# A layer of recurrent-memory attention and SwiGLU on one core: earlier stack loads, an up sum in SBUF, and x operands split anew

## The chip, the cores and the metric

The kernel runs on one core of one Trainium2 chip, as one launch. The metric is the device time of that launch in microseconds. The core has the engines PE (TensorE, with its weight loader PEld), DVE (VectorE), ACT (ScalarE), POOL (GpSimd) and SP, which here only issues DMA transfers. All transfers of this kernel are issued by SP, in program order. Every engine works through its own list of instructions in order and waits on semaphores. Tiles lie in SBUF, the results of matmuls in eight banks of PSUM.

## The reference

The input x has 2048 rows of D = 576. Two branches are mixed by a gate of each row:

```python
g = _sigmoid((x * gate_w).sum(-1, keepdims=True))
a = _A_ref(x, A_wq, A_wk, A_wv, A_wo, A_beta)
b = _B_ref(x, B_w_gate, B_w_up, B_w_down)      # (silu(x @ w_gate) * (x @ w_up)) @ w_down
return g * a + (1 - g) * b
```

The attention branch has 32 heads of 18 and 4 segments of 512 rows. In each segment a head does causal softmax attention inside the segment and reads a memory matrix of the earlier segments:

```python
logits = einsum(qs, ks) * scale + mask;  a_dot = softmax(logits) @ vs
a_mem = (phi(qs) @ M) / (phi(qs) @ z + 1e-6)
o = g * a_mem + (1 - g) * a_dot
M = M + phi(ks).T @ vs;  z = z + phi(ks).sum()
```

The SwiGLU branch goes from 576 to 4608 = 36 x 128 and back. All is in float32.

## The kernel before, in words

**Number formats.** A float32 operand is split into a high part and the rest (`split`, L106: a copy on ACT, a subtraction on DVE), and a product is three matmuls of such parts. In attention, q and k are split into three bfloat16 parts, which are stacked along the contracted dimension.

**Three stages.** The first (L263 to L574) does the projections, segment by segment: `qk` (9 chains each), `v_step` and the memory. What it makes is stored to DRAM: the stacked q and k (`stk`), v (`vd`), the memory's part (`med`). It also stores, for segments 0 and 1, the split operands of x: four tiles of high and low part in segment 0, two in segment 1 (`xd`, L547, six stores of 128x1024 float32) and the remainder rows (`xsd`). The third stage (from L1045) does the output projection and the mixture.

**The second stage** interleaves two things by hand. The outer loop (L942) runs over 72 blocks: two halves of the rows (the first half takes segments 2 and 3, the second segments 0 and 1) by 36 blocks of 128 hidden columns. Between the products of a block stands `tick()`, eight to a block, which calls `beat`. A beat first runs what `defer` put down for it (`due`: loads, splits, stores), then up to three groups of the down product (`down_group`), then, when enough credit has been gathered, one step of attention (`next(att)`).

**A block's gate and up product** (L984 to L1019) use a scheme with seven products in place of eight: each of `XO[0]` to `XO[6]` is one operand of x, a block of x or a sum of such blocks, split in high and low part, of two tiles z = 0, 1 (hence fourteen). Three PSUM banks hold the sums: `a` (bank 0), `xx` (bank 1), `y` (bank 2). The rows `p5`, `sg0` and `sg1` are SBUF tiles of 128x512 from a pool of four. The first up block is added on DVE at L994 (into bank 2, on which PE goes on), the second at L1011 (again a new tile in bank 2). At the block's end `sg1` (second block: up sum times Silu of the gate) is multiplied at L1015 and `sg0` at L1016, where `xx` comes straight from PE. The next block's first product goes to bank 0, its copy to bank 1 and its second product to bank 2. The rows are then split to `hh`, `hl` (L1017, L1018), the operands of the down product. Every third block starts 48 groups of the down product over the last three blocks; each is nine matmuls of 288 columns into one of two banks, and a DVE addition into `ya` (L788).

**Attention steps.** `att_gen` (L713) runs 64 units (a segment and a pair of heads) of five steps. Step n of unit u does `s_bank(u, n)` (scores for the maximum, L619, reduced on DVE, L626), and for a unit two to three before it `t_bank` (L659, scores again with the maximum stacked in; exponential on ACT, L663; mask on POOL, L671), then a split of the probabilities (`p1` on DVE, L737, `p2` on POOL, L739) and `pv_step` (L688, L690). A unit's stacked q and k are ten loads (`stack_loads`, L171) into one of four buffers `qst`, `kst`: the first six bring what step 0 of the unit reads, the last four (pr = 1) what step 1 reads besides. They are issued for unit u + 1 in steps 2, 3 and 4 of unit u, three, three and four of them (L723). The row maxima go through DRAM: stored in step 3 (`mxd`, L720), loaded two units later in step 0 (`row_load`, L188).

**Weights.** In the first half each block's weights are loaded raw, summed and split (`w_make`), and stored (`wc`, `rc`); in the second half `w_fetch` loads them split (L599, L603).

**Between the halves** stand ten beats with the last 16 groups. From block 34 on, `x_second` (L890) makes the operands of the second half: eight raw tiles of x are loaded (L897) into a pool of four buffers, four operands for each z are summed on POOL in place (`total`) and split (`parts`), and three for each z (0, 3, 5, the plain blocks of x) are loaded split from `xd` (`kept`, L911). The remainder rows come from `xsd` (`rest`, L915). Each entry has the beat at which it runs, counted from the first tick of block 35.

Of the kernel before, what the change touches and what calls it, by code (L numbers as in the profile page):

```python
# [12 lines left out]
F32 = mybir.dt.float32  # L13
# [7 lines left out]
P = 128  # L21
# [4 lines left out]
L = 512  # L26
# [25 lines left out]
def f32(ap):  # L52
    return ap.bitcast(F32)
# [3 lines left out]
def gated_mix(ctx, tc, xT, wf, wd, wv, wo, beta, cmask, ident, bmask, out):  # L57
# [11 lines left out]
    mxd = dram.tile([2 * NB, 3, 8, P], BF, name="mxd")  # L69
    wc = dram.tile([FT, 7, P, 4 * P], F32, name="wc")  # L70
    rc = dram.tile([FT, 2, P, 2 * P], F32, name="rc")
    xd = dram.tile([2, 4, P, 2 * L], F32, name="xd")
    xsd = dram.tile([2, P, L], F32, name="xsd")
    dc = dram.tile([FT, P, 2 * D], F32, name="dc")
    ffd = dram.tile([8, P, D], F32, name="ffd")
# [30 lines left out]
    def split(hi, lo, src):  # L106
        nc.scalar.activation(hi, src, AF.Copy)  # L107
        nc.vector.tensor_sub(lo, src, f32(hi))  # L108
# [154 lines left out]
    with ExitStack() as st:  # L263
# [228 lines left out]
        for s in range(NSEG):  # L492
# [47 lines left out]
            for n in range(8):  # L540
                hf, i = divmod(n, 4)
                flush()
                v_step(s, hf, i)
                if s:
                    mem_step(s, n // 2, n % 2)
                if s < 2 and n > 1 and n - 2 in ((0, 1, 2, 3), (2, 3))[s]:
                    late.append((xd[s, n - 2], f32(xs_of[s][0][n - 2]).rearrange("p a b -> p (a b)")))  # L547
                if s < 2 and n == 6:
                    late.append((xsd[s], f32(xs_of[s][1])))
                if s < 3:  # L550
                    if n == 0:
                        xs_of[s + 1] = x_tiles(s + 1)
                    if 1 <= n < 6:
                        x_split(xs_of[s + 1], n - 1, raws["x", n - 1])
                else:
                    if n == 4:
                        wraw_of[1] = [w_load(1, u) for u in range(2)]
                    if n < 2:
                        first_sum(6, n)
                    elif n < 6:  # L560
                        nc.gpsimd.memset(kst[n - 2], -1.0)
                    else:
                        nc.gpsimd.memset(mbs[n - 6], 0.0)
                    if n > 2:
                        for z in stack_loads(0)[2 * n - 6:2 * n - 4]:
                            nc.sync.dma_start(*z)
                    for _ in range((0, 0, 2, 3, 3, 3, 3, 3)[n]):
                        if start[0][0] < 8:
                            start.pop(0)[1]()
# [7 lines left out]
    with ExitStack() as st:  # L577
# [135 lines left out]
        def att_gen():  # L713
            N = 10 * NB
            for tau in range(N + TL + VL + 4):
# [4 lines left out]
                    nc.sync.dma_start(mxd[u - 1].rearrange("z q n -> q z n"), mts.pop(u - 1))  # L720
                if n == 0 and 2 <= u <= 2 * NB + 1:
                    row_load(u - 2)
                if n > 1 and u + 1 < 2 * NB:  # L723
                    for d in stack_loads(u + 1)[(0, 3, 6)[n - 2]:(3, 6, 10)[n - 2]]:
                        nc.sync.dma_start(*d)  # L725
                z = tau - TL - VL - 1
                if z % 20 == 0 and 0 <= z < N and z // 20 + 1 < 4 * NSEG:
# [162 lines left out]
        def x_second(new, xs):  # L890
            r = {}
            todo = []

            def load(z, q):
                b, kt = ((0, z), (1, z), (0, 2 + z), (1, 2 + z))[q]
                r[z, q] = raw_tile()[:, :L]
                nc.sync.dma_start(r[z, q], xT[HALF[1][b], :, kt])  # L897

            def total(z, j):
                c, d, e, g = (r.get((z, q)) for q in range(4))  # L900
                o, p, q = {1: (c, d, c), 4: (d, g, d), 2: (g, g, c), 6: (e, e, g)}[j]
                nc.gpsimd.tensor_sub(o, p, q)

            def parts(z, j):
                new[j][z] = x_slot(SLOT[j], z)
                split(new[j][z][:, 0], new[j][z][:, 1], r[z, {1: 0, 4: 1, 2: 3, 6: 2}[j]])

            def kept(z, j):
                b, kt = {0: (0, z), 3: (0, 2 + z), 5: (1, 2 + z)}[j]
                new[j][z] = x_slot(SLOT[j], z)  # L910
                nc.sync.dma_start(f32(new[j][z]).rearrange("p a b -> p (a b)"), xd[b, kt])  # L911

            def rest(b):
                xs[b] = xs_tile()
                nc.sync.dma_start(f32(xs[b]), xsd[b])  # L915

            for z, loads, sums, splits in ((0, (-3, -2, 5, 4), (4, 7, 8, 8), (5, 9, 9, 10)),
                                           (1, (9, 10, 12, 11), (13, 13, 14, 14), (14, 15, 15, 16))):
                todo += [(o, lambda z=z, q=q: load(z, q)) for o, q in zip(loads, range(4))]
                for o, p, j in zip(sums, splits, (1, 4, 2, 6)):  # L920
                    todo += [(o, lambda z=z, j=j: total(z, j)), (p, lambda z=z, j=j: parts(z, j))]
                todo += [(o + z, lambda z=z, j=j: kept(z, j)) for o, j in ((6, 0), (12, 3), (14, 5))]
            todo += [(16 + b, lambda b=b: rest(b)) for b in range(2)]
            return sorted(todo, key=lambda t: t[0])

        def seven(t, w, x, first, last):
# [15 lines left out]
        for pos, (half, f) in enumerate(seq):  # L942
# [64 lines left out]
            nc.scalar.activation(sg1, y, AF.Silu)  # L1007
            tick()
            rest2(a, wr[1], XS[1])
            y = y_tile()  # L1010
            nc.vector.tensor_add(y, a, p5)  # L1011
            tick()
            seven(xx, w[6], XO[6], False, False)
            rest2(xx, wr[1], XS[0])
            nc.vector.tensor_mul(sg1, y, sg1)  # L1015
            nc.vector.tensor_mul(sg0, xx, sg0)  # L1016
            defer(2, lambda t=(hh[:, 0], hl[:, 0], sg0): split(*t))  # L1017
            split_by(3, hh[:, 1], hl[:, 1], sg1)  # L1018
            tick()  # L1019
# [99 lines left out]
```

## Time and profile before

Three runs took 1901.53, 1901.6 and 1904.46 us; the median is 1901.6. The profile is of one more execution.

| | |
|---|---|
| median of three runs | 1901.6 us |
| the profiled execution | 1898.35 us |
| its span | 1896.5 us |
| mean granted PE clock | 0.995 |
| busy ACT and POOL | 958.4 and 854.6 us |
| DMA: moved, mean rate | 337.63 MB, 178 GB/s |
| share of 16 DMA engines, SP's queue | 54.0% |

The span runs from the first to the last instruction; the profiled execution's own time has 1.85 us more around it. Matmuls are pipelined and their ends are modelled, so a matmul of 512 columns shows 0.39 us and the next starts 0.23 us behind it. A row of a timeline has the start, the time until the end of the last of the merged instructions, engine, line, operation, output and input, the count, and in brackets how long the engine stood idle ahead of it and who ended that. A row of waits has the waiting engine, tile and line, the one waited for, the total in us, the number of times and the longest. "PEld" is the loader of PE's weights, which works ahead of the matmuls; "SPq" is the issue of a transfer.

By stage, the projections end at about 230 us, the first half runs to about 1027 us, the second to about 1806 us, and the output projection to the end.

### The profile page before, as it was taken

Reading aid. Unit: us, or ns where it says so; the run is one execution under the profiler, and the core shown is the slowest. Engines: PE = TensorE matmul, PEld = TensorE weight load, DVE = VectorE, ACT = ScalarE, POOL = GpSimd, SP = SyncE. Lnnn points to the kernel's source line nnn. Section 1 sums busy time; section 2 is a strip of 40 time slices with the busy share of each in tenths; the row PEclk is TensorE's granted clock in tenths of the full one; section 3 lists DMA queues with packets and bytes.
Section 4 is the critical chain, followed back from the end, with each engine's and each line's share of the span. In section 5 each row is a group of like instructions: output and inputs, shape, how many; then the busy total and the mean of one; then the engine's idle time right before and its main releaser. Section 6 shows DMA issues by size and latency. Waiting matters only on the chain.

```text
span 1896.5 us, 36496 instructions
## 1 busy us (share of the span) xinstructions
PE 1820.1 (96%) x12508; PEld 1544.5 (81%) x12508; DVE 1217.4 (64%) x3026; ACT 958.4 (51%) x1778; POOL 854.6 (45%) x1246
## 2 busy tenths in 40 slices
PE   8999999999999999999998999999999999999999
PEld 7889877887887888788777788878778878888899
DVE  5555677777767777877676566565556555655455
ACT  7666556456546656664663553544454354354311
POOL 3323623554555464555446454454444444444121
PEclk9999999999999999999999999999999999999999
DMA  6544586456446646654757653554464364445544
GB/s 237 197 171 167 186 282 216 146 190 227 155 162 224 209 150 204 229 171 145 234 178 255 196 169 112 165 167 131 144 186 138 120 194 145 136 149 155 191 151 137
DMA packets 206472, 337.63 MB, mean 178 GB/s; under 512 B 38416, under 2 KB 95888, under 8 KB 206288
## 3 DMA queue, kind: packets, MB, share of 16 engines
q1 hardware_dynamic: 206288, 335.32, 54.0%
q8 instruction: 99, 1.62, 0.4%
q14 instruction: 85, 0.70, 0.1%
HBM read 197.48 MB, written 137.76 MB: 177 GB/s over the span
## 4 chain that ended last, share of the span: by engine, by line
PE 70%; DMA 10%; DVE 7%; ACT 5%; issue 3%; SPq 3%; POOL 1%; DVEq 0%; ACTq 0%; POOLq 0%
PE bank L783 23%; PE bank L930 21%; PE bank L130 11%; PE bank L936 4%; PE bank L619 3%; PE bank L659 3%; DMA kst<-stk 2%; SPq L725 2%; PE bank L688 2%; DMA raw<-in_wf_dram 1%; PE bank L690 1%; DMA qst<-stk 1%; DMA qst<-mxd 1%; ACT L663 1%; DMA woraw<-in_wo_dram 1%
## 5 line engine op out<-in xcount | busy, mean ns | idle before, releaser
L739 POOL TENSOR_TENSOR p<-pe,p 128x512 f16<-128x512 f32 x320 | 372.9, 1165 | 696.3 <-DVE p L737 607.6
L783 PE MATMUL bank<-dw,hh 128*128 128x288 f32 x2304 | 482.1, 302 | 11.4 <-DVE ya L788 7.4
L783 PEld LDWEIGHTS bank<-dw,hh 128*128 128x128 f32 x2304 | 378.7, 189 | 32.9 <-DVE ya L788 13.9
L663 ACT ACTIVATE pe<-bank 128x512 f32<-128x512 f32 x320 | 191.1, 597 | 356.5 <-PE bank L659 301.9
L783 PE MATMUL bank<-dw,hl 128*128 128x288 f32 x1152 | 340.7, 296 | 0.4 <-DVE hl L108 0.3
L788 DVE TENSOR_TENSOR ya<-bank,ya 128x288 f32<-128x288 f32 x352 | 160.1, 456 | 236.3 <-PE bank L783 234.1
L626 DVE CUSTOM_DVE_ANT_0 scr<-bank,cm 128x512 bf16<-128x512 f32 (+3 forms) x512 | 247.4, 483 | 23.3 <-PE bank L619 16.5
L783 PEld LDWEIGHTS bank<-dw,hl 128*128 128x128 f32 x1152 | 217.4, 189 | 0.8 <-DVE hl L108 0.8
L659 PE MATMUL bank<-qst,kst 111*128 111x512 bf16 (+3 forms) x512 | 151.6, 305 | 7.6 <-DMA qst<-mxd 7.6
L619 PE MATMUL bank<-kst,qst 108*128 108x512 bf16 (+3 forms) x512 | 126.4, 300 | 28.5 <-DMA kst<-stk 11.6
L737 DVE CAST p<-pe 128x512 f16<-128x512 f32 x320 | 151.8, 475 | 0.3 <-POOL pe L671 0.3
L671 POOL TENSOR_SCALAR_AFFINE_SELECT pe<-pe 128x256 f32<-128x256 f32 (+1 forms) x320 | 134.5, 420 | 15.2 <-ACT pe L663 12.5
L1011 DVE TENSOR_TENSOR bank<-bank,row 128x512 f32<-128x512 f32 x72 | 50.3, 699 | 108.3 <-ACT row L1007 107.7
L998 ACT ACTIVATE row<-bank 128x512 f32<-128x512 f32 x72 | 43.0, 597 | 132.6 <-PE bank L936 132.3
L663 ACT ACT_TABLE_LOAD x66 | 84.7, 1283 | 49.2 <-PE bank L659 48.3
L108 DVE TENSOR_TENSOR hl<-row,hh 128x512 fp32r<-128x512 f32 x72 | 50.3, 699 | 79.7 <-ACT hh L107 79.7
L130 PE MATMUL bank<-xo,qhi 128*128 128x512 f32 x288 | 92.3, 401 | 5.2 <-ACT xo L107 5.0
L619 PEld LDWEIGHTS <-qst 108*128 108x128 bf16 x512 | 50.3, 99 | 54.5 <-issue 34.1
L659 PEld LDWEIGHTS <-kst 111*128 111x128 bf16 x512 | 47.8, 97 | 50.0 <-issue 33.0
L1002 ACT ACTIVATE bank<-bank 128x512 f32<-128x512 f32 x72 | 41.9, 582 | 91.3 <-PE bank L930 87.8
L1004 ACT ACT_TABLE_LOAD x67 | 86.0, 1283 | 1.2
L320 POOL TENSOR_TENSOR q<-qr,q 128x512 bf16<-128x512 f32 x36 | 43.8, 1217 | 92.8 <-ACT q L319 86.1
(2085 smaller groups left out, 4230.5 us busy)
## 6 DMA issues: line engine op xcount, KB each, us to landing
raw<-in_wf_dram SPq DMA_DIRECT2D x72, 320.0 KB
dc<-dw SPq DMA_DIRECT2D x36, 576.0 KB
dw<-dc SPq DMA_DIRECT2D x36, 576.0 KB
stk<-q SPq DMA_DIRECT2D x32, 384.0 KB
draw<-in_wd_dram SPq DMA_DIRECT2D x36, 288.0 KB
vd<-vps SPq DMA_DIRECT2D x8, 912.0 KB
v<-vd SPq DMA_DIRECT2D x16, 456.0 KB
qst<-stk SPq DMA_DIRECT2D x128, 54.0 KB
```

Of the source, the lines that this page charges most:

```text
L130: nc.tensor.matmul(t, st[n], mv[n], start=(n == 0), stop=(n == 13))
L619: nc.tensor.matmul(t[:, c:c + w], qs[:KR, pr, P * i:P * i + P], ks[:KR, pr, 0:w], start=True, stop=True)
L626: nc.vector.tensor_tensor_reduce(scr[:, :w], t[:, c:c + w], cm[:, L - w:L], 1.0, -3.0e38, OP.add, OP.max, m[:, k:k + 1])
L659: nc.tensor.matmul(t[:, c:c + w], ks[:KR + 3, pr, P * j:P * j + P], qs[:KR + 3, pr, P * j:L], start=True, stop=True)
L663: nc.scalar.activation(pe, t, AF.Exp, scale=SCALE)
L671: nc.gpsimd.affine_select(d, d, pattern=pat, compare_op=OP.is_ge, fill=0.0, base=0, channel_multiplier=-1)
L737: nc.vector.tensor_copy(p1, pe)
L739: nc.gpsimd.tensor_sub(p2, pe, p1)
L783: nc.tensor.matmul(t, p, q[:, cs], start=(n == 0), stop=(n == 3 * CH - 1))
L788: nc.vector.tensor_add(ya[:, i, cs], t, ya[:, i, cs])
L930: nc.tensor.matmul(t, w[:, p, z], x[z][:, q], start=first and n == 0, stop=last and n == 5, skip_group_check=True)
L1004: nc.scalar.activation(sg0, sg0, AF.Silu)
```

## The change

Three edits, in one diff (whole but for context lines):

1. The ten stack loads of a unit are issued in two steps instead of three: six in step 2, four in step 3.
2. The second up block is summed in its own SBUF row (`p5`, in place of a new tile in bank 2), and at the block's end the product of `sg0` (gate times up from PE's bank) is made first, that of `sg1` second; the latter reads two SBUF rows.
3. The six stores to `xd` and the six loads from it are gone; operands 0, 3 and 5 of the second half are split from the raw tiles like the others. Their splits stand ahead of the sums that overwrite the raw tiles, the beats of sums and splits are set anew, three raw loads of z = 1 come one beat later, and the two remainder loads two beats earlier.

```diff
-    xd = dram.tile([2, 4, P, 2 * L], F32, name="xd")
...
-                if s < 2 and n > 1 and n - 2 in ((0, 1, 2, 3), (2, 3))[s]:
-                    late.append((xd[s, n - 2], f32(xs_of[s][0][n - 2]).rearrange("p a b -> p (a b)")))
...
-                if n > 1 and u + 1 < 2 * NB:
-                    for d in stack_loads(u + 1)[(0, 3, 6)[n - 2]:(3, 6, 10)[n - 2]]:
+                if n in (2, 3) and u + 1 < 2 * NB:
+                    for d in stack_loads(u + 1)[6 * (n - 2):4 * n - 2]:
                         nc.sync.dma_start(*d)
...
             def parts(z, j):
                 new[j][z] = x_slot(SLOT[j], z)
-                split(new[j][z][:, 0], new[j][z][:, 1], r[z, {1: 0, 4: 1, 2: 3, 6: 2}[j]])
-
-            def kept(z, j):
-                b, kt = {0: (0, z), 3: (0, 2 + z), 5: (1, 2 + z)}[j]
-                new[j][z] = x_slot(SLOT[j], z)
-                nc.sync.dma_start(f32(new[j][z]).rearrange("p a b -> p (a b)"), xd[b, kt])
+                split(new[j][z][:, 0], new[j][z][:, 1], r[z, (0, 0, 3, 2, 1, 3, 2)[j]])
...
-            for z, loads, sums, splits in ((0, (-3, -2, 5, 4), (4, 7, 8, 8), (5, 9, 9, 10)),
-                                           (1, (9, 10, 12, 11), (13, 13, 14, 14), (14, 15, 15, 16))):
+            for z, loads, steps in ((0, (-3, -2, 5, 4), ((1, -1, 0), (3, 1, 0), (4, -1, 1), (7, 4, 0), (7, -1, 5),
+                                                         (8, -1, 3), (8, 2, 0), (9, 6, 0), (9, -1, 4), (10, -1, 2),
+                                                         (10, -1, 6))),
+                                    (1, (9, 11, 13, 12), ((12, -1, 0), (13, 1, 0), (14, 4, 0), (14, -1, 1), (14, -1, 5),
+                                                          (15, 2, 0), (15, -1, 3), (15, -1, 4), (16, 6, 0), (16, -1, 2),
+                                                          (17, -1, 6)))):
                 todo += [(o, lambda z=z, q=q: load(z, q)) for o, q in zip(loads, range(4))]
-                for o, p, j in zip(sums, splits, (1, 4, 2, 6)):
-                    todo += [(o, lambda z=z, j=j: total(z, j)), (p, lambda z=z, j=j: parts(z, j))]
-                todo += [(o + z, lambda z=z, j=j: kept(z, j)) for o, j in ((6, 0), (12, 3), (14, 5))]
-            todo += [(16 + b, lambda b=b: rest(b)) for b in range(2)]
+                for o, j, k in steps:
+                    todo.append((o, lambda z=z, j=j: total(z, j)) if j > 0 else (o, lambda z=z, k=k: parts(z, k)))
+            todo += [(14 + b, lambda b=b: rest(b)) for b in range(2)]
...
             rest2(a, wr[1], XS[1])
-            y = y_tile()
-            nc.vector.tensor_add(y, a, p5)
+            nc.vector.tensor_add(p5, a, p5)
             tick()
             seven(xx, w[6], XO[6], False, False)
             rest2(xx, wr[1], XS[0])
-            nc.vector.tensor_mul(sg1, y, sg1)
             nc.vector.tensor_mul(sg0, xx, sg0)
+            nc.vector.tensor_mul(sg1, p5, sg1)
```

On PE the list of instructions stays as it is. DVE and ACT get six instructions more each, SP has twelve transfers fewer.

## The prediction

> **What bounds the kernel now.** I read the page first, then the waits of PE and of its weight loader, then the order of time around three places that the change touches.
>
> ```profile
> span 1896.5 us, 36496 instructions
> PE 1820.1 (96%) x12508; PEld 1544.5 (81%) x12508; DVE 1217.4 (64%) x3026; ACT 958.4 (51%) x1778; POOL 854.6 (45%) x1246
> ```
>
> The profiled execution took 1898.35 us, its span 1896.5 us and 1.85 us around it. PE is busy for 1820.1 us of that, and the change leaves its 12508 matmuls alone, so what can move are the 76.4 us in which PE waits. Who ends those waits (total us, times, longest):
>
> ```profile
> PE bank L619 <- DMA kst<-stk: 11.6, 11, 2.1
> PE bank L619 <- ACT pe L663: 10.9, 14, 2.1
> PE bank L659 <- DMA qst<-mxd: 7.6, 3, 6.5
> PE bank L783 <- DVE ya L788: 7.4, 8, 2.2
> ...
> PE bank L930 <- DVE bank L994: 4.3, 9, 1.1
> ...
> PE bank L619 <- DMA wc<-wo__11212: 3.4, 1, 3.4
> PE bank L930 <- DVE bank L1011: 3.0, 4, 1.5
> ...
> PE bank L619 <- DMA wo__20455<-wc: 1.8, 1, 1.8
> ...
> PE bank L619 <- ACT row L998: 0.7, 1, 0.7
> ```
> ```profile
> PEld bank L930 <- DVE bank L1011: 14.8, 26, 1.9
> ```
>
> No engine bounds the kernel as a whole beside PE; it is many small late arrivals. The largest is the stack (kst) that comes late to L619, and of those that the other two edits can reach, L1011 and the row load qst<-mxd are the next. 72 executions of the SwiGLU block, 36 to each half, share the time with 64 attention units of five steps.
>
> **The up row.** At the end of a block:
>
> ```profile
> 307.64 1.52 PE L930 MATMUL bank<-xo,wo__3382 128*128 128x512 f32 x6
> ...
> 308.38 0.58 ACT L1007 ACTIVATE row<-bank 128x512 f32<-128x512 f32 x1
> ...
> 308.99 0.70 DVE L1011 TENSOR_TENSOR bank<-bank,row 128x512 f32<-128x512 f32 x1 [2.00 <-ACT row L1007]
> 309.00 0.61 PE L936 MATMUL bank<-xs,wr__3385 128*128 128x512 f32 x2
> ...
> 309.75 1.66 PE L930 MATMUL bank<-xo,wo__3437 128*128 128x512 f32 x6
> ...
> 309.93 0.68 DVE L1015 TENSOR_TENSOR row<-bank,row 128x512 f32<-128x512 f32 x1
> ...
> 310.53 0.68 DVE L1016 TENSOR_TENSOR row<-bank,row 128x512 f32<-128x512 f32 x1
> ```
> ```profile
>   ACT row L1007: 107.7, 49
> ```
>
> L1011 writes its sum over the bank that the gate's Silu (L1007) still reads, so DVE stands there for 107.7 us in 49 blocks. The next block's first product overwrites bank 0, which L1011 reads, so PE waits for it too. Six matmuls take 1.52 us and two 0.61, so they follow each other by 0.23; behind the two of 309.00 L930 could start at 309.45 and starts at 309.75: 0.30 us lost. With the sum in its SBUF row, L1011 waits only for the matmuls into bank 0. They stand on PE right ahead of the product of 307.64, so they are done by about 307.9, a microsecond before the Silu; the sum then ends at 308.6 and no PE wait is left. The row is held to the block's end; the next to write its buffer is the next block's L998, behind three more products: nothing. Size: 3.0 us is all that shows as idle PE, 14.8 us as idle weight loader, which overstates because matmuls run on behind it. 26 cases: some sixteen like the one above at 0.30 make 4.8, two long ones (1.9 the longest) add 3. I take **-8**, range -3 to -15. What is late next is the gate times up: the first product waits for PE's last matmul as before, the second, which used to lie in front of it under PE's work, now comes behind it.
>
> **The stack loads.** SP issues loads for unit u+1 in steps 2, 3 and 4 of unit u, and L619 reads the last four in step 1 of u+1:
>
> ```profile
> 1195.79 0.29 SPq L720 DMA_DIRECT2D mxd<-mt  x1
> ...
> 1202.41 0.72 SPq L725 DMA_DIRECT2D qst<-stk  x1
> 1203.17 0.69 SPq L725 DMA_DIRECT2D kst<-stk  x1
> ...
> 1204.57 0.61 SPq L725 DMA_DIRECT2D kst<-stk  x1
> ```
> ```profile
> 1209.44 0.38 PE L619 MATMUL bank<-kst,qst 108*128 108x512 bf16 x1 [1.44 <-DMA kst<-stk]
> ```
>
> All ten wait at their start for the buffer, which L659 of step 1 reads last; six instead of three now stand behind that one wait. The last issue ends at 1205.18, PE is released 4.26 us later and had been ready 1.44 us before. After the change the four follow the mxd store of step 3. Steps 2 and 3 issue three and one more (0.7 us each), so mxd goes from 1195.79 to about 1198.0 and the four end near 1201.1; landed 4.26 us later, 1205.3, against 1208.0 when PE wants them: 2.7 us to spare. I take the 11 kst waits to be of this shape, and, as the same matmul waits in them, the 3.4, 1.8 and 0.7 us put down to weight transfers and to L998, which no L619 reads. Together 17.5; I take **-15**, range 0 (the queue of transfers, not the issue, sets the landing) to -17.5. What moves behind them: SP is in order, so weights, raw rows and row loads queued between come up to 2.2 us later. The slack of one such weight:
>
> ```profile
> 1182.42 0.36 SPq L599 DMA_DIRECT2D wo__15635<-wc  x1
> ```
> ```profile
> 1190.12 1.63 PE L930 MATMUL bank<-xo,wo__15635 128*128 128x512 f32 x6
> ```
>
> 7.3 us from the issue's end to its use, less 2.2 leaves 5.1, over the 4.26 of the stack. I charge **+1**, range 0 to 8.
>
> **Between the halves.** Six stores (0.5 MB each) in the projections and their six loads between the halves go; six splits come, one ACT and one DVE instruction each, and loads of raw x stay (three of them one step later).
>
> ```profile
> 992.24 1.00 SPq L911 DMA_DIRECT2D xo<-xd  x2
> ...
> 995.03 0.30 SPq L189 DMA_DIRECT2D qst<-mxd  x1
> ```
> ```profile
> 1002.63 0.58 PE L659 MATMUL bank<-qst,kst 111*128 111x512 bf16 x1 [6.51 <-DMA qst<-mxd]
> ```
> ```profile
> 990.00:1000.00 10.00, 4.00 (x23) 2.68 (x22) 5.67 (x10) 4.64 (x7) 3.92 (x4) 0.97 0.93 281
> 1000.00:1010.00 10.00, 7.37 (x41) 6.54 (x41) 6.95 (x17) 2.90 (x6) 7.83 (x12) 0.69 0.89 295
> ```
>
> The columns are length, PE, PEld, DVE, ACT, POOL busy, clock, DMA share, GB/s. The row load stands behind two xd loads, 1.05 MB at 281 GB/s: 3.7 us of its landing are theirs, so -3.7 of the 6.51. The stores fall in the projections (L130), for which the list of waits has no transfer: nothing. Against it, the splits:
>
> ```profile
> L108 DVE TENSOR_TENSOR xo<-raw,xo x8: 674/1002/1215, 991.0 to 1021.9; 128x512 fp32r<-128x512 f32 x8
> ```
>
> Six more at 1.0 us make 6.0 on DVE, which is busy 12.6 us of those 20, so they fit on average; but the adds of the down product (L788) free PE's two banks and stand in the same queue, and the new ACT splits stand ahead of the hh split, waiting for raw x. I charge +2.7: net **-1**, from -5 to +6.
>
> **The clock.** PE's granted clock falls after a wait:
>
> ```profile
> 862.00:866.00 4.00, 1.08 (x8) 0.99 (x9) 3.42 (x8) 0.50 (x2) 2.61 (x4) 1.00 0.84 285
> 866.00:870.00 4.00, 4.00 (x15) 3.33 (x14) 0.49 (x3) 0.25 (x2) 2.51 (x7) 0.57 0.49 181
> ```
>
> This is the 3.4 us wait, then 4 us at 0.57: 4 x 0.43 = 1.7 lost. That wait should go; the dip at 1000 to 1010 (0.69, 3.1 us, part of it while PE stood) may shorten. **-2**, range 0 to -5.
>
> **The price of the new product and its order.** The product of the up row now reads two SBUF rows. Rows for that:
>
> ```profile
> L1015 DVE TENSOR_TENSOR row<-bank,row x72: 677/685/692, 237.2 to 1803.5; 128x512 f32<-128x512 f32 x72
> ```
> ```profile
> L869 DVE TENSOR_TENSOR hl<-row,hh x72: 676/682/1224, 244.6 to 1806.3; 128x512 fp32r<-128x512 f32 x72
> ```
> ```profile
> 656.08 0.41 DVE L233 TENSOR_TENSOR wo__8285<-raw,wo__8285 128x256 fp32r<-128x256 f32 x1
> ...
> 656.97 1.16 POOL L739 TENSOR_TENSOR p<-pe,p 128x512 f16<-128x512 f32 x1 [1.57 <-DVE p L737]
> ...
> 657.36 1.06 DVE L233 TENSOR_TENSOR wo__8296<-ws,wo__8296 128x256 fp32r<-128x256 f32 x1
> ```
>
> From bank and row it took 677 to 692 ns in all 72 blocks; a subtraction of two SBUF rows has the same median, 682, but reached 1224. The same instruction took 0.41 us alone and 1.06 us while POOL's L739 ran, ending 0.29 us after it. So the new product costs 0.68 us, and up to 1.16 more where it meets POOL. DVE finishes the block's pair up to 0.68 later than today where it now waits for PE. That reaches PE only in the 24 blocks with down-product groups, whose adds follow; elsewhere DVE has the microsecond it gained at L1011. I charge **+1.5**; bounds 0 and 24 x (0.68 + 1.16) = 44.
>
> The Trainium skill, page "SBUF — State Buffer", section "Who interferes with whom", says that a DVE instruction with two SBUF inputs contends with a GpSimd instruction that reads SBUF, and that whoever comes second is blocked for the whole instruction. By that rule, the trace's 1.06 us agrees, and this edit moves an operation from the safe side to the other; it is the slower rival below.
>
> **The sum.** Waits removed come back in part: PE, no longer held, meets the next late one, chiefly the exponentials (ACT pe L663, 10.9 us, untouched). I give back a quarter of the row's and the stack's 23: +5.5, bounds 0 and 23. So -8 - 15 + 1 - 1 - 2 + 1.5 + 5.5 = **-18**. On the profiled execution's 1898.35 that is 1880.4; the median of the three runs, 1901.6, lies 3.25 above it, so 1883.6, say **1883.5 us**, 1.0% faster. Likeliest range 1875 to 1893. Under 0.2% (3.8 us) a measurement here can't tell from no change.
>
> **Rivals.**
> - *The waits move on*: the whole 23 returns at ACT's exponentials, or the stack lands no earlier because transfers queue (DMA share 0.93 in one stretch) and the row's -8 alone stays. The first gives -18 + 17.5 = -0.5, so 1901; the second -18 + 15 - 3.75 (its share of what was given back) + 1.7 (the clock dip stays), -5, so 1896.5. For it: 10.9 us of such waits at L619. Against: ACT is 51% busy, and the example has 2.7 us to spare. 0.16.
> - *DVE late behind the block's end* (slower): the new product, behind the one that waits for PE and blocked by POOL, delays the adds after it, so PE waits for its two banks. All 24 blocks at 1.84 make +44 for the +1.5: -18 + 42.5 = +24.5, so 1926. It decides against the change from (18 + 1.5) / 24 = 0.81 us per block. For it: 7.4 us of L783 waits for L788 today, and the 1.06 above. Against: the product of two rows has median 682, and POOL is 45% busy. 0.10.
> - *More than the sum*: nothing returns, the clock dips go, the boundary gains its 3.7: -8 - 17.5 - 3.7 - 5 = -34, so 1867. 0.08.
>
> **How the numbers follow.** Forecast 0.66. The first rival's 0.16 is 0.07 for 1896.5 (0.27% faster), 0.08 for 1901 and 0.01 above. So faster 0.66 + 0.08 + 0.07 = 0.81, within 0.2% 0.08, slower 0.10 + 0.01 = 0.11. The range, 1867 to 1899, leaves out the slower rival, the top of the first and little below.
>
> **What would show it.** Right: the kst wait of L619 near zero with loads in two groups of six and four; DVE's 107.7 us at L1007 gone and no PE wait for the up sum; PE's wait between the halves under 4 us. Wrong: the up product's median well over 700 ns or L788 waits over 15 us (second rival); L619's waits for ACT grown by ten (first); weights late at L930; a longer stretch between the halves. If the stack waits go but the time stays, my reading of L619 as PE's own loss is wrong.

## The result: 1880.8 us against 1901.6 us

| | before | after |
|---|---|---|
| median (runs) | 1901.57 us (4) | 1880.76 us (4) |
| lowest to highest | 1899.64 to 1904.46 | 1876.04 to 1885.42 |
| ratio, 95% interval | | 0.9889 [0.9861, 0.9917] |
| profiled execution, span | 1898.35, 1896.5 | 1885.42, 1883.6 |
| DMA moved | 337.63 MB | 331.34 MB |

The forecast was 1883.5 us and faster; the time lies 2.7 us below it and inside the range. Measured again beside the experiments, the same kernel took 1883.74 us, 0.9917 [0.9893, 0.994] of before. The profiled execution of after is the slowest of its four, so its trace shows 12.9 us of gain (1898.35 to 1885.42), not the 20.8 of the medians.

The page of after, its first lines:

```profile
span 1883.6 us, 36500 instructions
PE 1816.2 (96%) x12508; PEld 1548.4 (82%) x12508; DVE 1227.2 (65%) x3032; ACT 960.4 (51%) x1784; POOL 858.9 (46%) x1246
```

PE waits for 1883.6 - 1816.2 = 67.4 us, before 76.4: 9.0 less. Its busy time fell by 3.9 us as well, with the same 12508 matmuls. The list of PE's waits in after (total us, times, longest us):

```profile
PE bank L616 <- ACT pe L660: 14.9, 17, 2.7
PE bank L780 <- DVE ya L785: 12.6, 11, 3.4
PE bank L925 <- DVE bank L989: 9.2, 8, 1.8
...
PE bank L780 <- DVE hl L107: 2.6, 2, 1.4
...
PE bank L656 <- DMA qst<-mxd: 1.1, 2, 0.6
```

(After's lines are one to six lower: L616, L656, L660, L780 and L785 were L619, L659, L663, L783 and L788; L925, L931, L989 were L930, L936, L994; the sum is L1005, the gate's product L1009, the up product L1010.) The kst row, 11.6 us, is not there any more; the row load fell from 7.6 to 1.1. DVE's wait of 107.7 us for the Silu is gone too. What grew: the exponentials 10.9 to 14.9, L989 4.3 to 9.2, ya 7.4 to 12.6. The end of the block that the prediction took as its example, in order of time:

```profile
307.62 0.69 DVE L1005 TENSOR_TENSOR row<-bank,row 128x512 f32<-128x512 f32 x1 [0.57 <-PE bank L931]
...
308.44 0.58 ACT L1002 ACTIVATE row<-bank 128x512 f32<-128x512 f32 x1
...
308.78 0.62 PE L931 MATMUL bank<-xs,wr__3377 128*128 128x512 f32 x2
...
309.23 1.52 PE L925 MATMUL bank<-xo,wo__3430 128*128 128x512 f32 x6
...
309.70 0.68 DVE L1009 TENSOR_TENSOR row<-bank,row 128x512 f32<-128x512 f32 x1
...
310.30 0.68 DVE L1010 TENSOR_TENSOR row<-row 128x512 f32<-128x512 f32 x1
```

The sum now runs before the Silu (L1002), and the next block's first product starts 0.45 us behind the two matmuls of 308.78, not 0.75 as before. The 0.30 is gone, and it had never shown as idle PE but as a busy matmul. The product of two SBUF rows over all blocks:

```profile
L1010 DVE TENSOR_TENSOR row<-row x72: 675/681/1219, 237.7 to 1791.0; 128x512 f32<-128x512 f32 x72
```

Its median is 681 ns, as forecast, and 1219 its longest.

Between the halves, the row load's 6.51 us wait went (by which edit, e1 and e3 below show), and others stand there:

```profile
992.25 3.38 POOL L899 TENSOR_TENSOR raw<-raw 128x512 f32<-128x512 f32 x2
992.74 1.75 DVE L107 TENSOR_TENSOR xo<-raw,xo 128x512 fp32r<-128x512 f32 x1
...
992.87 0.61 PE L780 MATMUL bank<-dw,hl 128*128 128x288 f32 x1 [1.43 <-DVE hl L107]
...
996.55 1.83 DVE L107 TENSOR_TENSOR xo<-raw,xo 128x512 fp32r<-128x512 f32 x2
...
999.89 0.85 PE L780 MATMUL bank<-dw,hh 128*128 128x288 f32 x2 [3.37 <-DVE ya L785]
```
```profile
990.00:1030.00 40.00, 35.14 (x232) 30.91 (x231) 30.16 (x65) 11.39 (x23) 26.65 (x32) 0.80 0.51 169
```
```profile
990.00:1030.00 40.00, 30.20 (x226) 26.48 (x225) 27.02 (x59) 12.81 (x23) 23.51 (x27) 0.91 0.85 281
```

The columns are those of the prediction's windows; the first row is after's, the second before's. The transfers are lighter (DMA share 0.51, before 0.85). But PE waits 3.37 us for DVE's adds, which stand in the queue with the splits, and the granted clock of these 40 us is 0.80, before 0.91.

**The clock as a term of its own.** PE runs at full speed or, in short stretches, at half; the granted clock is the mean over the span. Each run lists its span and its mean granted clock. In four sets of runs of before the mean is 0.9944 (29 runs), 0.9943 (14), 0.9945 (17) and 0.9946 (8), so it belongs to a kernel and is not chance alone. I split each time into span x clock, called the time at full clock here, and the rest, the loss to the clock; both are means over all runs of a kernel, against before on the same chip. The standard error of a full-clock mean is 0.4 to 0.9 us (1.3 for the whole change), so a difference between two rows of the table is uncertain by about 1 us, more where the whole change is one of them.

| kernel | ratio of times, 95% | full clock, us | clock loss, us |
|---|---|---|---|
| e1 stack loads alone | 0.9952 [0.9935, 0.9968] | -10.2 | +0.2 |
| e2 row sum and gate first alone | 0.9963 [0.9948, 0.9979] | -6.7 | -0.2 |
| e3 x operands alone | 1.0018 [1.0001, 1.0035] | +1.7 | +1.9 |
| e4 stack and e2 | 0.9926 [0.9901, 0.9952] | -15.4 | +1.0 |
| r2 the same again | 0.992 [0.9898, 0.9942] | -16.5 | +0.6 |
| r1 whole change again | 0.9917 [0.9893, 0.994] | -16.6 | +0.2 |
| e5 stack, row sum, up first | 0.9944 [0.9926, 0.9962] | -13.9 | +2.7 |
| e8 stack, bank sum, gate first | 0.9918 [0.9899, 0.9938] | -12.9 | -3.4 |
| e6 whole, x steps spread | 0.989 [0.9868, 0.9912] | -19.3 | -2.4 |
| e10 e6 with the sum in its bank | 0.9905 [0.9889, 0.992] | -15.4 | -3.0 |
| e7 whole, ten loads in one step | 1.0024 [1.0007, 1.0041] | -5.2 | +9.6 |
| e9 whole, loads a step later | 1.0101 [1.0077, 1.0125] | +9.5 | +8.9 |

### The profile page after: what moved, and what is told of

It is laid out like the page before. It is cut to its first block, busy times and chain, and to the rows that moved or that the text cites. A ratio compares the mean times of both kernels' runs of the same rounds, so it can differ in the third digit from the quotient of the medians.

```text
span 1883.6 us, 36500 instructions
## 1 busy us (share of the span) xinstructions
PE 1816.2 (96%) x12508; PEld 1548.4 (82%) x12508; DVE 1227.2 (65%) x3032; ACT 960.4 (51%) x1784; POOL 858.9 (46%) x1246
## 2 busy tenths in 40 slices
DMA packets 204744, 331.34 MB, mean 176 GB/s; under 512 B 38224, under 2 KB 95696, under 8 KB 204560
## 4 chain that ended last, share of the span: by engine, by line
PE 80%; DVE 6%; DMA 5%; ACT 4%; issue 3%; SPq 1%; POOL 1%; DVEq 0%; ACTq 0%; POOLq 0%
PE bank L925 28%; PE bank L780 23%; PE bank L129 11%; PE bank L931 5%; PE bank L656 3%; PE bank L616 3%; PE bank L685 2%; PE bank L687 1%; ACT L660 1%; SPq L722 1%; PE bank L363 1%; DVE xo L107 1%; ACT pe L660 1%; PE bank L409 1%; DMA qst<-mxd 1%
## 5 line engine op out<-in xcount | busy, mean ns | idle before, releaser
L780 PE MATMUL bank<-dw,hh 128*128 128x288 f32 x2304 | 485.9, 303 | 16.8 <-DVE ya L785 12.6
L780 PEld LDWEIGHTS bank<-dw,hh 128*128 128x128 f32 x2304 | 381.5, 190 | 39.6 <-DVE ya L785 20.0
L660 ACT ACTIVATE pe<-bank 128x512 f32<-128x512 f32 x320 | 191.0, 597 | 342.1 <-PE bank L656 304.4
L780 PE MATMUL bank<-dw,hl 128*128 128x288 f32 x1152 | 342.5, 297 | 2.6 <-DVE hl L107 2.6
L785 DVE TENSOR_TENSOR ya<-bank,ya 128x288 f32<-128x288 f32 x352 | 159.9, 455 | 224.9 <-PE bank L780 223.6
L623 DVE CUSTOM_DVE_ANT_0 scr<-bank,cm 128x512 bf16<-128x512 f32 (+3 forms) x512 | 247.1, 483 | 17.5 <-PE bank L616 10.8
L780 PEld LDWEIGHTS bank<-dw,hl 128*128 128x128 f32 x1152 | 219.0, 190 | 3.2 <-DVE hl L107 3.2
L656 PE MATMUL bank<-qst,kst 111*128 111x512 bf16 (+3 forms) x512 | 151.8, 305 | 1.1 <-DMA qst<-mxd 1.1
L616 PE MATMUL bank<-kst,qst 108*128 108x512 bf16 (+3 forms) x512 | 126.3, 300 | 15.0 <-ACT pe L660 14.9
L656 PEld LDWEIGHTS <-kst 111*128 111x128 bf16 x512 | 47.9, 97 | 53.2 <-issue 37.4
L1005 DVE TENSOR_TENSOR row<-bank,row 128x512 f32<-128x512 f32 x72 | 49.7, 690 | 59.2 <-PE bank L931 59.1
L1009 DVE TENSOR_TENSOR row<-bank,row 128x512 f32<-128x512 f32 x72 | 49.6, 689 | 48.0 <-PE bank L931 43.2
```

Of the source, the lines that this page charges most:

```text
L616: nc.tensor.matmul(t[:, c:c + w], qs[:KR, pr, P * i:P * i + P], ks[:KR, pr, 0:w], start=True, stop=True)
L623: nc.vector.tensor_tensor_reduce(scr[:, :w], t[:, c:c + w], cm[:, L - w:L], 1.0, -3.0e38, OP.add, OP.max, m[:, k:k + 1])
L656: nc.tensor.matmul(t[:, c:c + w], ks[:KR + 3, pr, P * j:P * j + P], qs[:KR + 3, pr, P * j:L], start=True, stop=True)
L660: nc.scalar.activation(pe, t, AF.Exp, scale=SCALE)
L780: nc.tensor.matmul(t, p, q[:, cs], start=(n == 0), stop=(n == 3 * CH - 1))
L785: nc.vector.tensor_add(ya[:, i, cs], t, ya[:, i, cs])
```

## The experiments

Each was measured beside before, on the same chip. The theory was that of the prediction: late stack loads and the up sum's wait for the Silu were what PE lost, and their removal adds up. The rivals: what is taken away returns at the next late engine; or the gain comes from another edit than the one that I named.

### e1, e2, e3: each edit alone; e4, r2: two together; r1: all three again

```diff
 e1
-                if n > 1 and u + 1 < 2 * NB:
-                    for d in stack_loads(u + 1)[(0, 3, 6)[n - 2]:(3, 6, 10)[n - 2]]:
+                if n in (2, 3) and u + 1 < 2 * NB:
+                    for d in stack_loads(u + 1)[6 * (n - 2):4 * n - 2]:
 e2
-            y = y_tile()
-            nc.vector.tensor_add(y, a, p5)
+            nc.vector.tensor_add(p5, a, p5)
...
-            nc.vector.tensor_mul(sg1, y, sg1)
             nc.vector.tensor_mul(sg0, xx, sg0)
+            nc.vector.tensor_mul(sg1, p5, sg1)
```

e3 is the rest of the change's diff, e4 and r2 are e1 and e2 together, r1 is the whole.

> The stack loads in two steps alone, all else as before. My theory (each edit is worth what its own wait was, less a quarter that returns): the waits of L619 for kst (11.6 us, with the mis-named ones 17.5) go to under 2, and the time falls by 10 to 12 us, to about 1891. Rival 1 (the waits move on to ACT's exponentials, 10.9 us before): kst goes but ACT pe at L619 grows by ten, time within 4 us of before. Rival 2 (the stack is all that the change has): it falls by the whole 20, to 1881.

> The up sum in its SBUF row and the gate product first, alone. My theory: L1011's wait for the Silu and PE's wait for L1011 (14.8 us of weight loader, 8 of time) go, two return, the new product costs 1.5: time down by 4 to 5 us, about 1897. Rival 1 (PE is held at the next DVE result of the block instead, L994, whose waits in the profile of after are 9.2 us where before had 4.3): within 2 us of before. Rival 2 (two SBUF inputs meet POOL): slower than before, the new product's median over 700 ns.

> No x operands in DRAM, all fourteen split anew, alone. My theory: -3.7 for the row load that no longer stands behind 1 MB, +2.7 for splits in front of others: within 3 us of before. Rival 1 (the extra splits delay hh and the down product's adds, as the profile of after hints: the stretch from block 35 to block 36 is 2.3 us longer there, with 17 us of half clock): slower by 3 to 6 us. Rival 2 (3 MB less to store and to load also help the projections): faster by over 5 us, and the projections end earlier.

> Stack loads and row, x operands still kept in DRAM: the change without its third edit. My theory, with the third edit worth about -3 with the clock: 1884 to 1887. Rival (the third edit costs, by the longer stretch between the halves): 1875 to 1880, faster than the whole change.

> Stack loads and row, without the third edit, once more, now beside the whole. My theory: 2 to 4 us faster than the whole, because the stretch between the halves keeps the x operands' 3 MB of transfers but not six splits on DVE. Rival (the third edit is worth its 3.7 when the other two are there, as the row load's wait of 2.4 us left in this kernel suggests): slower than the whole by 3 us or more.

> The whole change as it stands, beside its variants on one chip. My theory now: the stack is worth 9, the row 7 (each alone beside before: 0.9952 and 0.9963), the x operands cost 3 (0.9981 the other way), so 13 to 15 us under before, ratio 0.992 to 0.993. Rival: the edits help each other (PE held by one late thing lets the next catch up) and the whole stays at the 0.989 of its first runs, 21 us under before.

e1 took 1888.2, e2 1891.22, e3 1901.55, e4 1884.59 (before 1898.9); r2 1884.38, r1 1883.74 (before 1899.68). The stack alone is worth 9 to 11 us and the kst row is gone from its list of PE's waits, which begins:

```profile
PE bank L619 <- ACT pe L663: 15.5, 16, 2.3
PE bank L783 <- DVE ya L788: 10.5, 12, 2.3
PE bank L130 <- ACT xo L107: 5.2, 1, 5.2
...
PE bank L930 <- DVE bank L994: 7.0, 9, 1.4
```

17.5 us were named as the stack's; PE's idle time fell from 76.4 to 67.2, by 9.2, since the first, second and last row here grew by 4.6, 3.1 and 2.7. The row load's wait went as well, from 7.6 to 0.8. The row edit alone gives 7.7 us of time, on top of the stack 3.6 (1884.59 for 1888.2). The x edit alone costs 1.7 us at full clock and 1.9 by the clock, and on top of the other two (r1 against r2) it changes nothing that these runs can tell.

The row load's wait between the halves was charged to the `xd` transfers. Who PE waits for, first in e1, which keeps them all, then in e3, which has none:

```profile
PE bank L659 <- DMA qst<-mxd: 0.8, 1, 0.8
```
```profile
PE bank L616 <- DMA dc<-dw: 6.5, 1, 6.5
```

So the stack's new place alone ends that wait (e4 and r2 keep 2.4 and 2.0 us of it there). In e3 the row load waits only 0.4, but a wait of the same size, 6.5, stands between the halves at L616, put down to a transfer that L616 doesn't read.

The traces also tell where along the kernel the time goes. From the first block's start to block 35's, e1 takes 754.5 us and before 754.8; from block 36's start to the end 861.0 and 869.5. So the stack's gain lies in the second half, where the blocks make no weights: every kernel here with six loads in step 2 and four in step 3 needs 857 to 864 us there, the three without (before, e2, e3) 869.5 to 879.9. e2 is the other way round: 740.1 us in the first stretch, but 879.9 in the second, where its kst waits are 11.2 us for 8.0. So part of what the row edit gains in the first half is lost to later stacks in the second. These are single traces (after and r1, the same kernel, differ by 3.7 us in the first stretch and 0.8 in the second), and why the row edit gains less there once the stack edit is in (750.8 us in e4, 751.7 in r2) is open.

### e5 and e8: the row edit taken apart

```diff
 e5, on e1
-            y = y_tile()
-            nc.vector.tensor_add(y, a, p5)
+            nc.vector.tensor_add(p5, a, p5)
...
-            nc.vector.tensor_mul(sg1, y, sg1)
+            nc.vector.tensor_mul(sg1, p5, sg1)
             nc.vector.tensor_mul(sg0, xx, sg0)
 e8, on e1
-            nc.vector.tensor_mul(sg1, y, sg1)
             nc.vector.tensor_mul(sg0, xx, sg0)
+            nc.vector.tensor_mul(sg1, y, sg1)
```

> Stack loads and the up sum in its row, but the products in the old order: up times Silu first, gate second. My theory (the sum's place is what frees PE; the order of the two products only moves 0.68 us on DVE): within 3 us of the stack and row kernel. Rival (the order matters: in the profile of after, ACT's copy L982 waits 21.1 us behind the product that now comes second): faster than it by over 3 us. Rival 2 (gate first frees bank 1 sooner and that is what PE gains): slower by over 3 us.

> Stack loads and the gate product first, but the up sum in its new tile of bank 2 as before, so that it still waits for the Silu. My theory (the wait for the Silu is what holds PE): PE's loader still waits about 14 us for L1011 and DVE about 100 us for L1007; time like the stack loads alone, ratio 0.994 to 0.996. Rival (the order of the two products is what the row edit gains, as the kernel with the old order, 0.9944, suggests against 0.992): 0.991 to 0.993, with L1011's waits in place.

e5, the sum in its row with the old order, took 1888.15 us, no different from e1's 1888.2. e8, on e1 only the order changed, took 1882.9, as fast as both together. Yet in e8 the wait that I had priced is all there. Who DVE's L1011 and PE's loader wait for in e8:

```profile
DVE bank L1011 <- ACT row L1007: 106.2, 49, 5.6
```
```profile
PEld bank L930 <- DVE bank L1011: 14.8, 26, 1.9
```

So in time it is the order that paid. At full clock, too, it is worth something: -2.7 us from e1 to e8, each against its own before, and -2.0 from e5 to r2 and e4. The gate's product reads bank 1, which the next block's copy (L987) overwrites, and it makes the row from which the next split starts. ACT's waits for it, first e1, then e8:

```profile
ACT bank L987 <- DVE row L1016: 7.4, 5, 2.3
ACT hh L107 <- DVE row L1016: 3.7, 2, 2.1
```
```profile
ACT hh L107 <- DVE row L1015: 2.5, 2, 1.6
ACT bank L987 <- DVE row L1015: 1.7, 1, 1.7
```

In these rows ACT waits 6.9 us less for the gate's product, which now lies at L1015, ahead of the other. It ends on average 1.01 us behind PE's last matmul for it, in e1 1.35 (r2 0.99, e5 1.30): 0.3 us sooner, not the whole 0.68 of a product. And PE waits less in e8 for three things, of which two are ACT's or come behind ACT (e1 15.5, 10.5 and 7.0):

```profile
PE bank L619 <- ACT pe L663: 12.0, 18, 1.8
PE bank L783 <- DVE ya L788: 8.8, 13, 2.3
...
PE bank L930 <- DVE bank L994: 4.7, 7, 1.3
```

Together -7.5 us; in all, PE's idle time falls from 67.2 us to 60.3. Against the account speaks one row: PE's wait for the copy itself, L987, is 3.3 us in e8 and 1.1 in e1. That the three rows follow from the earlier copy and split is argued, not shown; the time of e8 is measured. (With the sum in its row, the copy's waits are put down to the up product instead: L982 for L1010, 21.1 us in nine waits in after. In all nine the matmuls that the copy reads end within 0.04 us of that product, so the copy could hardly have begun earlier.)

At full clock the sum's place is worth something after all: e1 to e5 -3.8 us, e8 to r2 and e4 (-15.9 on average) -3.0. Between the starts of L936's last matmul and L930's next, the traces of e1 and e8 have, outside stretches of lower clock, 17 and 18 intervals of 0.4 to 0.6 us where 0.23 would do, those of e5 and r2 two and one; that is the 0.30 of the prediction's example, some sixteen times. But e5 loses 2.7 us more to the clock than before, e1 0.2 and e8 -3.4, and in time nothing is left.

### e6 and e10: the x steps spread, and the sum back in its bank

```diff
 e6, on the whole change
-            for z, loads, steps in ((0, (-3, -2, 5, 4), ((1, -1, 0), (3, 1, 0), (4, -1, 1), (7, 4, 0), (7, -1, 5),
-                                                         (8, -1, 3), (8, 2, 0), (9, 6, 0), (9, -1, 4), (10, -1, 2),
-                                                         (10, -1, 6))),
-                                    (1, (9, 11, 13, 12), ((12, -1, 0), (13, 1, 0), (14, 4, 0), (14, -1, 1), (14, -1, 5),
-                                                          (15, 2, 0), (15, -1, 3), (15, -1, 4), (16, 6, 0), (16, -1, 2),
+            for z, loads, steps in ((0, (-3, -2, 3, 1), ((1, -1, 0), (3, 1, 0), (4, -1, 1), (5, 4, 0), (5, -1, 5),
+                                                         (6, -1, 3), (6, 2, 0), (7, 6, 0), (7, -1, 4), (8, -1, 2),
+                                                         (9, -1, 6))),
+                                    (1, (7, 8, 10, 9), ((11, -1, 0), (12, 1, 0), (12, -1, 5), (13, -1, 1), (13, 4, 0),
+                                                        (14, -1, 3), (14, 2, 0), (15, -1, 4), (15, 6, 0), (16, -1, 2),
 e10, on e6
-            nc.vector.tensor_add(p5, a, p5)
+            y = y_tile()
+            nc.vector.tensor_add(y, a, p5)
...
-            nc.vector.tensor_mul(sg1, p5, sg1)
+            nc.vector.tensor_mul(sg1, y, sg1)
```

Each entry of `steps` is (beat, operand to sum or -1, operand to split). The whole change has three steps in each of the beats 14 and 15 and up to two in 7 to 10; e6 starts them earlier and has at most two in a beat.

> The whole change with the third edit's beats set otherwise: the raw loads of z = 0 three and one beats earlier, splits and sums of z = 0 in beats 1 to 9 where they stood in 1 to 10, those of z = 1 one or two per beat from 11 on. My theory (DVE was too full in the two short beats behind block 35: adds of the down product and the split of hh stood behind four splits of x, PE waited 3.4 and 1.4 us and its clock fell): PE's wait for L785 there under 1 us, half clock 7 us or less where it was 17, and 3 to 5 us faster than the whole. Rival (the raw loads come earlier into a full queue and weights or row loads are late instead): no faster.

> The fastest so far, the whole change with its x steps spread (0.989 of before), but with the up sum put back into bank 2, the gate product still ahead of the up product. Theory: the place of the sum is worth nothing, the order of the two products is what paid; then the sum waits again for the gate's Silu (L1003, some 106 us of DVE waits in 49 blocks), the weight loader shows some 15 us of waits for the sum's bank at L931, and the time stays at 0.987 to 0.991. Rival, the prediction's own term: the Silu's wait on the sum costs PE its 3 to 8 us; then 0.9905 to 0.9935, with some 3 us of PE waits for the sum at L931 and the sum of PE's idle time up by as much. A gain beyond 0.987 is expected by neither.

e6 took 1878.36 us beside 1883.74 for the whole change (r1). From block 35's start to block 36's it needs 2.6 us less than before, r1 0.1 less, and after's profiled execution 2.3 more; e10 2.7 less. e6's window between the halves, and its wait for ya over the whole span:

```profile
990.00:1030.00 40.00, 37.78 (x253) 32.95 (x253) 30.17 (x70) 14.92 (x28) 25.89 (x33) 0.89 0.60 196
```
```profile
PE bank L780 <- DVE ya L785: 9.4, 11, 2.3
```

PE is busy 37.78 of these 40 us (after 35.14) at a clock of 0.89 (0.80). Of the 9.4 us for ya 0.2 lie between the halves, where after has 3.4; the half-speed stretch there is 10.24 us long, where I had expected 7 or less. So once the splits don't come in a bunch, the x edit gains about 2.5 us there (e6 46.1 us from block 35 to 36, e4 and r2 48.4 and 48.6). The rest of the 5.4 us lies outside these blocks, and by the table half of the 5.4 is clock (-2.4 for +0.2); what causes that is open. In the total time the spreading isn't shown to pay: e6's 0.989 [0.9868, 0.9912] overlaps r1's 0.9917 [0.9893, 0.994], and the first four runs of the whole change had 0.9889.

e10 took 1880.62 us, 0.9905 against e6's 0.989. The intervals overlap, so the time doesn't decide between the theories; at full clock the sum's place is worth -3.8 here, the third time that a size of 3 to 4 us comes out, and the waits say where it goes. PE's waits of e10:

```profile
PE bank L616 <- ACT pe L660: 12.8, 16, 3.1
PE bank L780 <- DVE ya L785: 5.7, 10, 1.2
...
PE bank L925 <- DVE bank L989: 4.1, 7, 0.9
...
PE bank L925 <- DVE bank L1006: 3.4, 6, 1.5
```

3.4 us are the sum's, and in e6 they are gone; but e6 waits 8.2 for L989, 9.4 for ya and 16.9 for the exponentials. PE's idle time is 57.3 us in e10 and 63.1 in e6.

### e7 and e9: when the stack loads are issued

```diff
 e7, on the whole change: all ten in step 2
-                if n in (2, 3) and u + 1 < 2 * NB:
-                    for d in stack_loads(u + 1)[6 * (n - 2):4 * n - 2]:
+                if n == 2 and u + 1 < 2 * NB:
+                    for d in stack_loads(u + 1):
 e9, on the whole change: six in step 3, four in step 4
+                if n in (3, 4) and u + 1 < 2 * NB:
+                    for d in stack_loads(u + 1)[6 * (n - 3):4 * n - 6]:
```

> The whole change with all ten stack loads in step 2 (where it has six in step 2 and four in step 3). My theory (once the loads land before PE wants them, earlier is worth nothing more): no kst wait at L616, time within 3 us of the whole (ratio about 0.992). Rival (a burst of ten in front of weights and row loads makes these late): 4 us or more over the whole, with waits of L925 for weights or of L656 for the row load.

> The whole change with the stack loads one step later: none in step 2, six in step 3, four in step 4. My theory (PE's waits at L616 follow from the time between issue and use): kst waits come back in step 1 as before the change, 11 to 20 us, perhaps some in step 0; time 9 to 15 us over the whole (ratio 0.997 to 1.000). Rival (the gain came from fewer steps with loads, so shorter bursts elsewhere on SP, not from the earlier issue): within 3 us of the whole.

e9 took 1918.36 us, 35 more than the whole change where I had expected 9 to 15, and brings the stack's wait back, with what SP stands for ahead of it:

```profile
PE bank L616 <- DMA kst<-stk: 18.8, 14, 2.4
```
```profile
SPq L717 <- POOL mt L637: 138.0, 34, 8.8
```

So the issue sets when the stack lands, and a late one costs PE. SP has no load to issue in step 2 and stands at the store of the maxima, behind which the loads now come; in before this row read 53.8, 27 and in after 23.4, 21.

e7 took 1903.53. I had held that earlier is worth nothing more; it costs 20 us against the whole change. kst waits for nothing in it. SP does, at the row load:

```profile
SPq L188 <- DMA mxd<-mt: 71.8, 36, 4.0
```
```profile
PE bank L616 <- ACT pe L660: 21.0, 16, 4.5
...
PE bank L925 <- ACT bank L982: 6.5, 4, 3.7
```

In after that row reads 1.0, 3, 0.5. The row load of step 0 needs the maxima stored in step 3, and that store now comes behind ten loads. Whatever SP has behind the row load waits along, the stores and loads of weights too. The profiled execution falls 9.8 us behind before by block 35 and gains 7 of them back in the second half, where the blocks make no weights. So the burst costs only in the first half; that it makes the weights late there is argued, and through which transfer it reaches ACT I haven't isolated.

## Why the prediction was right, and which step was wrong

The forecast of -18 us is 16.0 without its clock term. At full clock r1 measured -16.6. The total is right in part by luck, as the terms show.

- **The stack loads**: the mechanism and the size are right, the sum behind the size is not. -15, +1 for SP's queue and its share of the waits that return (a quarter of 15) make -10.25; e1 measured -10.2 at full clock. But e1 also ended the row load's wait, 6.8 us of which the forecast had given 3.7 to another edit, and more came back than it held (last point). Whether the issue or the queue of transfers sets the landing was the open end of its range; e9 shows that it is the issue. The first rival failed in both forms: the waits at the exponentials grew by 4.0 us, not by ten, and the stack did land earlier.
- **The up row**: the mechanism is there and the step is too large. -8 and a quarter back is -6; measured -3.0 to -3.8 at full clock. The sixteen cases of 0.30 went, as sized. The 3 us that I added for "two long ones" did not: the intervals of over 1 us between those matmuls are six in e1 and six in e5. In time the place of the sum moved the ratio by -0.0008 (e1 to e5), +0.0002 and +0.0008 (e8 to r2 and e4) and -0.0015 (e10 to e6), each within the intervals: by the rows and the table above, waits at L994 and the clock took the rest.
- **The price of the new product and its order**: this is the step that failed. It charged +1.5 for the new product and for the gate's product going first, as a delay of the other. Measured for the order: -2.7 (e1 to e8) and -2.0 (e5 to r2 and e4) at full clock, each uncertain by about 1 us, and -5.3 and -3.6 to -3.8 us in the medians. I followed only who waits for the pair's end, and not who waits for the first of the two: bank 1 and the split of `sg0` come free 0.3 us sooner on average. The term's other half, that the product itself costs little, held: 50.3 us of busy time for L1010's 72 products against 49.4 for the up product of before.
- **DVE late behind the block's end** (the slower rival): failed. The median stayed at 681 ns; ya rose to 12.6 us, under the 15 set as the sign, and 3.4 of them are the one wait between the halves.
- **Between the halves**: -1 forecast, -0.6 measured (r1 against r2 and e4, full clock, less than its error), alone +1.7. The reading behind -3.7 is wrong: the row load's wait ends with the stack edit and all `xd` transfers in place (e1, 0.8 us), and 2.0 to 2.4 us are what e4 and r2 left of it. With the splits spread, e6 needs 2.6 us less than before there; bunched, they took back 2.5 (r1) to 4.9 (after), where I had charged 2.7. After's splits, fourteen now:

```profile
L107 DVE TENSOR_TENSOR xo<-raw,xo x14: 679/827/1751, 977.3 to 1021.2; 128x512 fp32r<-128x512 f32 x14
```

  In the eight of before the longest was 1215. The one of 1.75 at 992.74 above runs beside POOL's two sums of together 3.38 us. The Trainium skill's rule (page "SBUF — State Buffer", section "Who interferes with whom"), that a DVE instruction with two SBUF inputs contends with a GpSimd instruction that reads SBUF, agrees with this row. At the block product, where I had made it a rival, 50.3 us for 49.4 is 0.9 us in all.
- **The clock**: -2 forecast, +0.2 measured for r1, -2.4 for e6. The wait of the row load went, but after's own boundary is slower (0.80); the dips follow other waits than the one that I looked at.
- **The waits that return**: +5.5 forecast. PE's idle time fell by 9.2 in e1 where 17.5 were named and 6.8 of the row load went besides, so 15.1 came back in other rows: 10.4 at L994, ya and the exponentials, as said. From block 36 on, where the time was gained, PE's idle time fell from 28.5 us to 20.4; in the first stretch it rose from 30.8 to 32.6. A quarter of all was not the rule in either.

So the total came out right with two errors of opposite sign in one edit (-6 for about -3.5, +1.5 for about -2.3), each of about 3 us, and with a stack term whose two errors also cancel. Only e5 and e8 show the first: the whole change and the three edits alone would have confirmed the wrong cause.

## What to carry to other kernels

Where two results leave an engine one behind the other, ask for each who waits for it, not only when the pair ends: the one that frees a bank for the next block was the better first here. A wait that a trace charges to one edit is tested by leaving the wait in and undoing the rest; here 106 us of DVE's waiting stayed and the kernel was as fast in time. In this kernel's DMA queue, which issues in order, the loads had a best place: all ten one step later cost 35 us, four of ten one step earlier 20. And read a gain by stages before it is called general: here the earlier loads paid only in the half where the blocks make no weights.

## What the runs showed that I had not expected

- Late arrivals are paid twice. Against the whole change, e7 loses 11.4 us at full clock and 9.4 to the clock, e9 26.0 and 8.8. Within the spans of the traces the clock stands at half speed in stretches together 37.5 and 41.2 us long (before 20.5, e6 17.1, in three stretches). A stretch is mostly 3.41 us long, 10.24 and 17.07 between the halves of e6 and after, and in before and after four of five each begin within 1.3 us behind a gap of 1.7 to 3.7 us between the starts of two matmuls. Nine other gaps of that length in before start none, so which waits do is not settled: e2, with 79.2 us of idle PE, loses no more than before with 76.4.
- PE's busy time holds waits too. Less half the length of the half-speed stretches, it is 1809 to 1813 us in the five traces with the sum in its bank (before, e1, e3, e8, e10) and 1801 to 1806 in the nine with the sum in the row, with the same 12508 matmuls.
